# A delta-rule recurrence with a gated MLP: transfers planned through one shared queue, and matmuls of zeros in TensorE's gaps before the first gate tile

## The chip, the core and the metric

The kernel runs on one core of a Trainium2 chip. The core has TensorE (PE, matmuls; its weight loads are shown apart as PEld), VectorE (DVE), ScalarE (ACT), GpSimd (POOL) and SyncE (SP), which here issues every transfer. Each engine runs its own list of instructions in order, and semaphores tie the lists together. The metric is the device time of one execution in microseconds. Three runs of the kernel before took 659.91, 661.75 and 661.90 us, a median of 661.75 us.

## The reference

For each of 32 heads a 48 by 48 state is carried over 768 tokens (a delta rule with normalized keys), and what it gives goes through a gated MLP:

```python
for t in range(S):                       # q, k, v: (4, 8, 768, 48), beta: (4, 8, 768)
    kt, vt, bt = (k_n[:, :, t], v[:, :, t], beta[:, :, t, None])
    y[:, :, t] = np.einsum('bhd,bhde->bhe', q[:, :, t], state)
    v_old = np.einsum('bhde,bhd->bhe', state, kt)
    state = state + bt[:, :, :, None] * np.einsum('bhd,bhe->bhde', kt, vt - v_old)
x = attn_out.transpose(0, 2, 1, 3).reshape(B * S, H * D)      # 3072 x 384
gate = 1.0 / (1.0 + np.exp(-(x @ w_gate)))                    # 384 x 1536
return (gate * (x @ w_val)) @ w_out                           # 1536 x 384
```

## The kernel before

The tokens are cut into 12 groups `g` of 64 (times 4 batches: 256 rows of the MLP). A group's recurrence is done by blocks. `gram` (L250, tile pg) multiplies keys with keys, and ACT copies the blocks out (G at L258, L at L263). `norms` (L199 to L232) is a chain of some twenty small DVE instructions that gives the keys' norms and the tile mq. `solve` or, for groups 0 and 1, `solve_halves` (L315) inverts a triangular system by a long DVE chain. For these two groups the halves are joined by two sets of 64 tiny matmuls, pz and pm (`joining`, L354): pz needs the DVE transposition into mt (L342), ACT copies pz out (`keep_z`, L365), pm multiplies again, and DVE subtracts pm from mt (L346). Then come three PE steps (pu at L406, pk at L399, pu again), with copies of the state rows su by DVE and ACT between them (L412, L414). Then come yy (L434, L437), the copies ys (L446, L448), the transposition pt (L476) and the copies xx (L482, L484) that feed the MLP. ACT also scales the values by mq (`scale_v`, L238, 16 instructions a group).

The MLP works on 144 tiles: 12 groups by 12 slices `f` of 128 columns of the hidden layer. A gate tile is 18 matmuls of 128x256 (`gate_val`, L494). ACT, DVE, ACT and DVE turn it into two halves h, and six matmuls of 128x384 (`outp`, L530) add it into po. The order of tiles is group 0 up to slice 5, group 1 whole, the rest of group 0, then the groups in turn.

The weights come as 36 pieces of 384 KB. Each piece, once it has landed, is converted by two ACT instructions (L165 and L170, tile raw), one DVE instruction (L182, tile u), one ACT cast (L187) and one DVE subtraction (L192, tile w). A piece is loaded (`load_piece`, L155) only when POOL has copied one word out of the piece six places before it (`mark`, L175), which waits for that piece's L170. All 36 are converted once and kept.

What order the engines' lists have is set by a planner in the kernel (`schedule`, L737). Every step is a task with an engine, a cost in ns, the tasks it waits for, and buffers it takes and frees. The planner goes through the tasks by the earliest start on an engine, takes among those that could start at nearly the same time the one with the longest chain behind it, and keeps its own clock. The instructions are then issued by planned start. A transfer is a task of SP: before, it was planned to land 2500 ns plus its size over 380 after it was issued, whatever else was on the way. PE tasks before the first gate tile were planned at 2.1 times their cost (`COLD`, L795).

Of the kernel before, what the change touches and what calls it, by code (L numbers as in the profile page):

```python
# [12 lines left out]
F32 = mybir.dt.float32  # L13
# [43 lines left out]
def deltanet_gated_mlp(ctx: ExitStack, tc: tile.TileContext, kd, qd, kv, beta, words, out):  # L57
# [295 lines left out]

    def joining(g, n):  # L354

        pool, tag = (ps_aux, "aux") if g else (ps_gv, "gv")
        state[g][n] = out = pool.tile([128, CP, 32], F32, name=f"{n}_{g}", tag=tag)
        lhsT, rhs = (scratch[:, 0], mt) if n == "pz" else (scratch[:, 1], scratch[:, 2])
        for c in range(CP):
            for r in range(0, 128, 32):  # L360
                nc.tensor.matmul(out=out[r:r + 32, c], lhsT=lhsT[r:r + 32, c], rhs=rhs[r:r + 32, c], start=True, stop=True)  # L361
# [187 lines left out]
    PE, DVE, ACT, POOL, SP = range(5)  # L549
    tasks, by_name = [], {}  # L550

    def task(name, engine, cost, fn, after=(), take=(), free=(), late=0, lands=0):

        t = dict(name=name, engine=engine, cost=cost, fn=fn, after=[by_name[a] for a in after], take=take, free=free, late=late, lands=lands, n=len(tasks))
        assert name not in by_name, name
        by_name[name] = t
        tasks.append(t)
        return name
# [21 lines left out]
    pools = dict(aux=2, seq=2, gv=2, po=2, G=1, gp=1, X=1, mt=1, scratch=1, row=3, ys=1, sg=3, h=3, u=3, kv=2, L=2, xa=0, xb=1, mq=1)  # L580
# [19 lines left out]
    def load(g, what):  # L600
        k = f"kq{g % 2}"
        if what == "k":
            transfer(f"dk{g}", lambda: load_k(g), 2, 400000, has(f"pk{g - 2}", f"pp{g - 2}"))
        if what == "q":
            transfer(f"dq{g}", lambda: load_q(g), 2, 524288, has(f"yy{g - 2}"))
        if what == "v":
            transfer(f"dv{g}", lambda: load_rows(g, 1), 2, 400000, has(f"pd{g - 2}", f"less{g - 2}.1.1"))
        if what == "t":
            transfer(f"dt{g}", lambda: load_rows(g, 0), 1, 393216, has(f"pd{g - 2}"))

    HALF = {0, 1}

    def recurrence(g):
# [15 lines left out]
        if half:  # L629
            task(f"X{g}", POOL, 520, lambda: clear(g), take=("X",))  # L630
            task(f"ll{g}", ACT, 750, lambda: lower_left(g), [got[5]], take=("scratch",), free=("G",))
            gen = solve_halves(g)
            costs = [285, 418] * 2
            for j in range(15, 0, -1):
                costs += [160 + 1.05 * 2 * (8 - j // 2) * j] * 2
            h = steps(f"h{g}", DVE, gen, costs, [n[-2]])
            by_name[h[3]]["free"] = ("gp",)
            e = steps(f"x{g}", DVE, gen, [180, 180], [h[-1], f"X{g}"])
            task(f"mt{g}", DVE, 712, lambda: next(gen), e[-1:], take=("mt",), free=("X",))
            task(f"pz{g}", PE, 1500, lambda: joining(g, "pz"), [f"mt{g}", f"ll{g}"], take=("gv" if g == 0 else "aux",))  # L640
# [68 lines left out]
    def out_of(i):  # L709
# [3 lines left out]
        if ends(g, f):  # L713
            cleared.clear()
            for s in range(NSUB):
                cleared.append(f"part{s}" if f < NF - 1 else f"res{g}.{s}")
                if f < NF - 1:
                    task(f"part{s}", ACT, 480, lambda s=s: keep_part(g, s), [f"out{i}"], free=("po",))
                else:
                    task(f"res{g}.{s}", DVE if g == 0 else ACT, 560 if g == 0 else 480, lambda s=s: result(g, s), [f"out{i}"] + (has(f"part{s}") if g == 0 else []), take=("row",), free=("po",))  # L720
                    transfer(f"st{g}.{s}", lambda s=s: store(g, s), 2, 100000, [f"res{g}.{s}"], free=("row",))

    half = constants()
    second_half(half)
# [12 lines left out]
    def schedule():  # L737
# [13 lines left out]
        order = []  # L751
# [7 lines left out]
        while len(order) < len(tasks):  # L759
# [38 lines left out]
    begun = []

    def warm(t):  # L800
        begun.extend([t] * t["name"].startswith("gate"))
        return bool(begun)
# [50 lines left out]
```

## Time and profile before

| | before |
|---|---|
| the profiled execution's own time | 662.25 us |
| its span, first to last instruction | 660.5 us |
| PE busy | 610.7 us (92%) |
| DVE busy | 475.9 us (72%) |
| ACT busy | 324.8 us (49%) |
| the chain that ended last | PE 85%, DMA 5%, DVE 3%, issue 3%, ACT 2% |
| first gate tile starts | 67.83 us |
| share of the 16 DMA engines, 10 to 30 us | 1.0 |

The busy share is an average of two stages: the one before the first gate tile, in which PE mostly waits, and the one after it, in which PE hardly ever does. The granted clock of TensorE has a column in the profile (1.00 is 2.4 GHz, 0.50 is 1.2 GHz). "issue" is time in which an engine waited for nothing that the profile shows.

### The profile page before, as it was taken

How to read it: one execution, taken by the hardware profiler on the slowest of the kernel's cores; microseconds unless marked ns; L12 is line 12 of the kernel's file. 1: busy time of each engine (PE TensorE's matmuls, PEld its weight loads, DVE VectorE, ACT ScalarE, POOL GpSimd, SP SyncE). 2: the span in 40 equal slices, each digit the busy share in tenths (PEclk: the TensorE clock that was granted, in tenths of full speed). 3: DMA queues.
4: the chain of work that ended last, by engine and by line, in shares of the span. 5: the costliest groups of instructions: out<-in, count | busy, mean ns of one | idle time of the engine just before them, and what ended most of it. 6: DMA issues, size and time to landing. Idle time of an engine off the chain costs nothing.

```text
span 660.5 us, 24130 instructions
## 1 busy us (share of the span) xinstructions
PE 610.7 (92%) x10504; PEld 588.1 (89%) x10504; DVE 475.9 (72%) x1482; ACT 324.8 (49%) x881; POOL 14.8 (2%) x57
## 2 busy tenths in 40 slices
PE   5135899999999999999999999999999999999996
PEld 4134899988999999999999999999999999999996
DVE  4947599995985985985985985985985985984221
ACT  5599787245444445445445445445345345344321
POOL 5011000000000000000000000000000000000000
PEclk9999799998999999999999999999999999999999
DMA  9969320021211211211211211211211210100101
GB/s 261 289 201 319 93 79 2 1 67 34 58 32 45 58 30 48 58 47 30 58 50 28 57 51 28 58 48 29 57 51 27 58 51 3 26 1 4 25 1 24
DMA packets 17769, 41.06 MB, mean 62 GB/s; under 512 B 4224, under 2 KB 7296, under 8 KB 17664
## 3 DMA queue, kind: packets, MB, share of 16 engines
q1 hardware_dynamic: 17664, 39.53, 21.4%
q8 instruction: 82, 1.34, 0.8%
q14 instruction: 23, 0.19, 0.1%
HBM read 34.80 MB, written 4.72 MB: 60 GB/s over the span
## 4 chain that ended last, share of the span: by engine, by line
PE 85%; DMA 5%; DVE 3%; issue 3%; ACT 2%; SPq 1%; POOL 0%; ACTq 0%; POOLq 0%
PE gv L494 46%; PE po L530 24%; DMA raw<-in_words_dram 3%; PE pu L406 3%; PE pp L274 2%; PE pk L376 2%; PE yy L434 2%; PE yy L437 2%; PE pg L250 2%; PE pk L399 1%; PE pd L457 1%; DMA kv<-in_kv_dram 1%; PE pt L476 1%; DMA kqp<-in_qd_dram 1%; DVE X L305 1%
## 5 line engine op out<-in xcount | busy, mean ns | idle before, releaser
L494 PE MATMUL gv<-xx,w 128*128 128x256 f32 x2592 | 333.0, 284 | 1.4 <-DVE sg L504 1.4
L494 PEld LDWEIGHTS gv<-xx,w 128*128 128x128 f32 x2592 | 325.7, 191 | 3.0 <-DVE sg L504 2.1
L530 PE MATMUL po<-w,h 128*128 128x384 f32 x864 | 181.5, 348 | 0.0
L530 PEld LDWEIGHTS po<-w,h 128*128 128x128 f32 x864 | 146.8, 189 | 3.6
L499 ACT ACTIVATE sg<-gv 128x256 f32<-128x256 f32 x144 | 55.0, 382 | 154.8 <-PE gv L494 154.7
L504 DVE TENSOR_TENSOR sg<-sg,gv 128x256 f32<-128x256 f32 x144 | 59.9, 416 | 81.5 <-ACT sg L499 81.2
L509 ACT CAST h<-sg 128x256 fp32r<-128x256 f32 x144 | 58.5, 407 | 93.7 <-DVE sg L504 92.8
L305 DVE TENSOR_TENSOR X<-X,tmp 128x126 f32<-128x126 f32 (+22 forms) x310 | 79.0, 255 | 9.2
L302 DVE TENSOR_TENSOR tmp<-X,gp 128x126 f32<-128x126 f32 (+22 forms) x310 | 78.2, 252 | 7.3
L514 DVE TENSOR_TENSOR h<-sg,h 128x256 fp32r<-128x256 f32 x144 | 60.0, 417 | 16.0 <-ACT h L509 15.1
L414 ACT COPY su<-pu 32x384 f32<-32x384 f32 x92 | 43.3, 471 | 18.8 <-PE pu L406 17.8
L238 ACT ACTIVATE kv<-kv,mq 128x48 f32<-128x48 f32 x192 | 46.8, 322 | 2.6 <-DVE mq L232 2.6
L279 DVE TENSOR_TENSOR kqp<-pp,pmask 64x512 f32<-64x512 f32 x48 | 32.0, 685 | 2.2 <-PE pp L274 1.9
L258 ACT COPY G<-pg 32x256 f32<-32x256 f32 (+1 forms) x72 | 26.5, 368 | 10.7 <-PE pg L250 9.4
L199 DVE STREAM_TRANSPOSE gp<-G 128x1024 f32<-128x1024 f32 x12 | 14.9, 1245 | 19.4 <-ACT G L258 19.4
L387 DVE TENSOR_TENSOR R<-kv,pk 128x384 f32<-128x384 f32 x44 | 22.4, 550 | 6.0 <-PE pk L399 2.8
L170 ACT ACTIVATE raw<-raw 128x384 f32<-128x384 f32 x36 | 18.6, 547 | 8.5 <-DMA raw<-in_words_dram 8.4
L466 DVE TENSOR_TENSOR su<-su,pd 48x384 f32<-48x384 f32 x40 | 22.1, 552 | 0.8
L361 PE MATMUL pz<-mt,scratch 32*32 32x32 f32 x256 | 4.5, 237 | 18.7 <-DVE mq L232 9.8
L192 DVE TENSOR_TENSOR w<-u,w 128x384 fp32r<-128x384 f32 x36 | 19.2, 551 | 3.3 <-ACT w L187 3.2
L250 PE MATMUL pg<-kqp 48*64 48x64 f32 x768 | 17.0, 241 | 4.5 <-DMA kqp<-in_kd_dram 4.5
L361 PEld LDWEIGHTS pz<-mt,scratch 32*32 32x32 f32 x256 | 4.0, 150 | 19.3 <-issue 17.2
(88 smaller groups left out, 469.1 us busy)
## 6 DMA issues: line engine op xcount, KB each, us to landing
raw<-in_words_dram SPq DMA_DIRECT2D x36, 384.0 KB, 5.2
kv<-in_kv_dram SPq DMA_DIRECT2D x24, 384.0 KB, 3.9
kqp<-in_qd_dram SPq DMA_DIRECT2D x24, 256.0 KB, 4.0
kqp<-in_kd_dram SPq DMA_DIRECT2D x24, 192.0 KB, 3.6
out_dram<-ot SPq DMA_DIRECT2D x48, 96.0 KB, 2.2
beta<-in_beta_dram SPq DMA_DIRECT2D x12, 16.0 KB, 3.7
```

Source lines behind the costliest of these rows:

```text
L238: nc.scalar.activation(V[:, c], V[:, c], AF.Copy, scale=mq[:, c, 0:1])
L250: nc.tensor.matmul(out=pg[e][t:t + 64, j], lhsT=kq[r:r + D, x, j], rhs=kq[r:r + D, x, j], start=True, stop=True)
L279: nc.vector.tensor_tensor(out=kq[t:t + 64, sec], in0=pp[e][t:t + 64], in1=pmask[t:t + 64, e].unsqueeze(1).to_broadcast([64, J, C]), op=ALU ...
L302: nc.vector.tensor_tensor(out=tmp, in0=X[:, k:16, j:j + 1].to_broadcast([128, n, j]), in1=gp[:, j:j + 1, 0:j].to_broadcast([128, n, j]), o ...
L305: nc.vector.tensor_tensor(out=X[:, k:16, 0:j], in0=X[:, k:16, 0:j], in1=tmp, op=ALU.add)
L414: nc.scalar.copy(su[r:r + 32, 3 if x else e], pu[0][r:r + 32])
L494: nc.tensor.matmul(out=pg[:, o], lhsT=parts[w, f][:, a, k * 128:(k + 1) * 128], rhs=x[b][:, k], start=(k == 0 and q == 0), stop=(k == KC - ...
L499: nc.scalar.activation(h, st["gv", f][:, 0], AF.Sigmoid)
L504: nc.vector.tensor_tensor(out=h, in0=h, in1=st["gv", f][:, 1], op=ALU.mult)
L509: nc.scalar.copy(hh[:, 0], st["sg", f])
L514: nc.vector.tensor_tensor(out=hh[:, 1], in0=st["sg", f], in1=hh[:, 0].bitcast(F32), op=ALU.subtract)
L530: nc.tensor.matmul(out=po[s], lhsT=hh[:, a, ts], rhs=parts["o", f][:, w], start=begins(g, f) and q == 0, stop=ends(g, f) and q == 2)
```

## The change

In the planner, SP's transfers now share one queue: a transfer lands at the later of the queue's last landing and 2400 ns after its issue, plus a load time of its own (1150 ns for a piece of weights, 1900 for keys, 2200 for queries). The factor `COLD` is gone. Up to the task gate0, wherever PE's planned clock stands more than `ROOM` (450 ns) before the next PE task, the planner puts in fills of 230 ns each. A fill is a bf16 matmul of 128x512 with its own weight load, both operands a broadcast zero, into a PSUM buffer of the tag gv that the gate tiles use later. So that this buffer is free, only one gv buffer is planned until gate0, and group 0's pm is written over its pz. No arithmetic of the result changes.

```diff
+    def warm_up():
+        if not hot:
+            hot.append(ps_gv.tile([128, 512], F32, name="warm", tag="gv"))
+        z = zero.bitcast(BF16)[:, 0:1]
+        nc.tensor.matmul(out=hot[0], lhsT=z.to_broadcast([128, 128]), rhs=z.to_broadcast([128, 512]), start=True, stop=True)
...
-        pool, tag = (ps_aux, "aux") if g else (ps_gv, "gv")
-        state[g][n] = out = pool.tile([128, CP, 32], F32, name=f"{n}_{g}", tag=tag)
+        st = state[g]
+        if g == 0 and n == "pm":
+            st["pm"] = st["pz"]
...
-    def transfer(name, fn, count, size, after=(), take=(), free=()):
-        return task(name, SP, 430 * count, fn, after, take=take, free=free, lands=2500 + size / 380)
+    def transfer(name, fn, count, load, after=(), take=(), free=()):
+        return task(name, SP, 430 * count, fn, after, take=take, free=free, lands=2400, load=load)
...
-        transfer(f"w{n}", lambda: load_piece(n), 1, 393216, pre)
+        transfer(f"w{n}", lambda: load_piece(n), 1, 1150, pre)
...
+            if e == PE and filling:
+                clock[e] = max(clock[e], READY)
+                while at - clock[e] > ROOM:
+                    between.append(dict(name="warm", fn=warm_up, start=clock[e], engine=PE, done=clock[e] + FILL))
+                    clock[e] += FILL
+                if t["name"] == "gate0":
+                    tokens["gv"].append(at)
+                    filling.clear()
...
-            cost = t["cost"] * (COLD if e == PE and not warm(t) else 1)
+            cost = t["cost"]
...
-            t["end"] = at + cost + LATENCY[e] + t["lands"]
+            t["end"] = at + cost + LATENCY[e]
+            if e == SP:
+                t["end"] = moved[0] = max(moved[0], at + t["lands"]) + t["load"]
...
+    READY, FILL, ROOM = 2500, 230, 450
```

The planner's new costs move instructions on PE, ACT and DVE. There are 122 fills in all. On PE, around the joining of group 0 (pg is group 1's gram, pu the first step after the joining), the list before was:

```order
L250 MATMUL pg_1_285<-kqp_77 64x64
L361 MATMUL pz_445<-mt,scratch 32x32 x64
L361 MATMUL pm_542<-scratch 32x32 x64
L406 MATMUL pu_0_0_649<-kv_126,mt 32x48 x2
L406 MATMUL pu_0_1_650<-kv_126,mt 32x48 x2
```

and PE's list at the same place is now this, with a pair of rows for each fill (47 between pg and pz, then 4 and 4):

```order
L259 MATMUL pg_1_304<-kqp_77 64x64
L201 LDWEIGHTS zero
L201 MATMUL warm<-zero 128x512
...
L375 MATMUL pz_492<-mt,scratch 32x32 x64
L201 LDWEIGHTS zero
L201 MATMUL warm<-zero 128x512
...
L375 MATMUL pz_492<-scratch 32x32 x64
```

The matmuls of the kernel stand in the same sequence; 55 fills stand among those shown. Before pz the list has 6, 13 and 47 of them; between the first pu and pk (L399 before, L413 now) there are 28, then 7 and 7, and at last 1 and 5 before group 1's pz. On ACT, ahead of the copy of group 0's pz into scratch, the list before ended with these rows (raw_6 to raw_9 are pieces of weights, kv_0 the values that are scaled):

```order
L170 ACTIVATE raw_6_321<-raw_6_321 128x384
...
L170 ACTIVATE raw_4_218<-raw_4_218 128x384
L165 ACTIVATE raw_4_218<-raw_4_218 128x384
L263 COPY L_1_283<-pg_1_0_284 32x256
L170 ACTIVATE raw_8_340<-raw_8_340 128x384
L170 ACTIVATE raw_9_348<-raw_9_348 128x384
...
L165 ACTIVATE raw_7_333<-raw_7_333 128x384
L238 ACTIVATE kv_0_126<-kv_0_126,mq_0_443 128x48 x16
L365 COPY scratch_86<-pz_0_445 128x512
```

and ACT's list before that copy is now:

```order
L165 ACTIVATE raw_4_231<-raw_4_231 128x384
L272 COPY L_1_302<-pg_1_1_304 32x256
L247 ACTIVATE kv_0_126<-kv_0_126,mq_0_490 128x48 x8
L379 COPY scratch_86<-pz_0_492 128x512
L247 ACTIVATE kv_0_126<-kv_0_126,mq_0_490 128x48 x8
L187 CAST w_0_657<-u_0_645 128x384
L322 ACTIVATE scratch_86<-G_1_301,under_85 128x16x16
L187 CAST w_1_697<-u_1_651 128x384
L428 COPY su_79<-pu_0_0_0_662 32x384 x2
L170 ACTIVATE raw_6_344<-raw_6_344 128x384
```

Pieces 6, 7, 8 and 9 are no longer converted ahead of the copy of pz but after the copies of su, and half of the scaling stands behind it. On DVE, around the subtraction of pm from mt (the row that writes mt), the list before was:

```order
L182 SCALAR_TENSOR_TENSOR u_1_535<-raw_1_134 128x384
L199 STREAM_TRANSPOSE gp_1_538<-G_1_282 128x1024
L203 TENSOR_SCALAR n1_1_610<-gp_1_538 128x32
...
L224 TENSOR_TENSOR nt_1_612<-m_1_614 128x32
L346 TENSOR_TENSOR mt_78<-mt_78,pm_0_542 128x512
L227 RECIPROCAL gam_1_647<-nt_1_612 128x32
```

and DVE's list there is now:

```order
L182 SCALAR_TENSOR_TENSOR u_1_651<-raw_1_141 128x384
L355 TENSOR_TENSOR mt_78<-mt_78,pz_0_492 128x512
L208 STREAM_TRANSPOSE gp_1_660<-G_1_301 128x1024
L212 TENSOR_SCALAR n1_1_702<-gp_1_660 128x32
...
L233 TENSOR_TENSOR nt_1_706<-m_1_706 128x32
L236 RECIPROCAL gam_1_751<-nt_1_704 128x32
```

The first 15 instructions of group 1's norms, which stood before the subtraction, now stand behind it and ahead of the copy of su. On SP the transfers stand in the same sequence up to piece 11; where a task had been planned elsewhere (piece 10 ahead of piece 12, the queries of group 2 after piece 26) it moves by a few places.

## Rows read from the trace of the kernel before

**Rows 1.** The page, part 1: busy time, share and instructions of PE.
```profile
PE 610.7 (92%) x10504; PEld 588.1 (89%) x10504; DVE 475.9 (72%) x1482; ACT 324.8 (49%) x881; POOL 14.8 (2%) x57
```

**Rows 2.** PE before gate0: start, length, line, tile, count [idle <-releaser].
```profile
6.71 1.90 PE L376 MATMUL pk<-su,kqp 48*64 48x48 f32 x62
...
11.21 1.87 PE L274 MATMUL pp<-kqp 48*64 48x64 f32 x59 [0.80 <-DMA kqp<-in_qd_dram]
...
12.88 2.42 PE L250 MATMUL pg<-kqp 48*64 48x64 f32 x63
25.09 1.50 PE L361 MATMUL pz<-mt,scratch 32*32 32x32 f32 x94 [9.78 <-DVE mq L232]
31.40 0.74 PE L361 MATMUL pz<-mt,scratch 32*32 32x32 f32 x34 [4.81 <-issue]
38.77 1.94 PE L361 MATMUL pm<-scratch 32*32 32x32 f32 x128 [6.63 <-ACT scratch L365]
...
45.83 1.99 PE L399 MATMUL pk<-su,L 32*32 32x48 f32 x64 [2.82 <-ACT su L414]
...
53.98 2.06 PE L434 MATMUL yy<-su,kqp 48*64 48x48 f32 x64 [3.50 <-ACT su L414]
55.97 1.95 PE L437 MATMUL yy<-su,kqp 128*64 128x48 f32 x32
...
67.49 0.42 PE L361 MATMUL pz<-mt,scratch 32*32 32x32 f32 x11 [2.18 <-issue]
67.83 4.21 PE L494 MATMUL gv<-xx,w 128*128 128x256 f32 x18
```

**Rows 3.** ACT before gate0, the same columns.
```profile
20.89 0.53 ACT L170 ACTIVATE raw<-raw 128x384 f32<-128x384 f32 x1
27.68 0.55 ACT L170 ACTIVATE raw<-raw 128x384 f32<-128x384 f32 x1 [6.25 <-DMA raw<-in_words_dram]
...
34.41 3.70 ACT L238 ACTIVATE kv<-kv,mq 128x48 f32<-128x48 f32 x16
38.13 0.59 ACT L365 COPY scratch<-pz 128x512 f32<-128x512 f32 x1
...
60.22 0.46 ACT L448 COPY ys<-yy 128x384 f32<-128x384 f32 x1
```

**Rows 4.** DVE around the subtraction of pm, the same columns.
```profile
29.39 1.24 DVE L199 STREAM_TRANSPOSE gp<-G 128x1024 f32<-128x1024 f32 x1
...
33.68 0.19 DVE L224 TENSOR_TENSOR nt<-m 128x32 f32<-128x32 f32 x1
40.77 0.69 DVE L346 TENSOR_TENSOR mt<-mt,pm 128x512 f32<-128x512 f32 x1 [6.89 <-PE pm L361]
...
43.11 1.14 DVE L412 COPY su<-pu 32x384 f32<-32x384 f32 x2
```

**Rows 5.** Stretches: length, busy PE, PEld, DVE, ACT, POOL, PEclk, DMA share, GB/s.
```profile
54.00:56.00 2.00, 2.00 (x66) 1.91 (x66) 1.69 (x9) 1.51 (x4) 0.17 (x1) 1.00 1.00 395
...
66.00:68.00 2.00, 0.51 (x12) 0.45 (x11) 0.00 (x0) 0.91 (x5) 0.00 (x0) 0.50 0.98 265
...
72.00:74.00 2.00, 2.00 (x153) 1.96 (x156) 1.16 (x3) 1.83 (x5) 0.12 (x1) 0.72 0.00 0
```

**Rows 6.** PE after gate0, the columns of the second group.
```profile
85.97 0.88 PE L406 MATMUL pu<-R,mt 32*32 32x48 f32 x64
...
90.15 1.15 PE L434 MATMUL yy<-su,kqp 48*64 48x48 f32 x64
91.23 1.14 PE L437 MATMUL yy<-su,kqp 128*64 128x48 f32 x32
...
98.36 4.48 PE L494 MATMUL gv<-xx,w 128*128 128x256 f32 x36
```

**Rows 7.** DMA queues, 28.5 to 29 us: packets, MB, share of 16 engines.
```profile
q8 instruction: 1, 0.02, 13.7%
```

**Rows 8.** A stretch of ten us after gate0, the columns of the fifth group.
```profile
90.00:100.00 10.00, 10.00 (x154) 9.76 (x154) 9.84 (x23) 7.78 (x21) 0.00 (x0) 1.00 0.18 55
```

More of the change, by code (lines that the diff above doesn't have):

```diff
@@ L192, in weight_lo @@
         nc.vector.tensor_tensor(out=t[:, 1], in0=us[n].bitcast(F32), in1=t[:, 0].bitcast(F32), op=ALU.subtract)
+    hot = []
+    def warm_up():
[3 more added lines that the diff above has]
+        nc.tensor.matmul(out=hot[0], lhsT=z.to_broadcast([128, 128]), rhs=z.to_broadcast([128, 512]), start=True, stop=True)
     def norms(g):
@@ L354, in joining @@
     def joining(g, n):
-        pool, tag = (ps_aux, "aux") if g else (ps_gv, "gv")
-        state[g][n] = out = pool.tile([128, CP, 32], F32, name=f"{n}_{g}", tag=tag)
+        st = state[g]
+        if g == 0 and n == "pm":
+            st["pm"] = st["pz"]
+        else:
+            pool, tag = (ps_aux, "aux") if g else (ps_gv, "gv")
+            st[n] = pool.tile([128, CP, 32], F32, name=f"{n}_{g}", tag=tag)
+        out = st[n]
         lhsT, rhs = (scratch[:, 0], mt) if n == "pz" else (scratch[:, 1], scratch[:, 2])
@@ L550, in deltanet_gated_mlp, with task @@
     tasks, by_name = [], {}
-    def task(name, engine, cost, fn, after=(), take=(), free=(), late=0, lands=0):
-        t = dict(name=name, engine=engine, cost=cost, fn=fn, after=[by_name[a] for a in after], take=take, free=free, late=late, lands=lands, n=len(tasks))
+    def task(name, engine, cost, fn, after=(), take=(), free=(), late=0, lands=0, load=0):
+        t = dict(name=name, engine=engine, cost=cost, fn=fn, after=[by_name[a] for a in after], take=take, free=free, late=late, lands=lands, load=load, n=len(tasks))
         assert name not in by_name, name
@@ L575, in steps @@
         return names
-    def transfer(name, fn, count, size, after=(), take=(), free=()):
-        return task(name, SP, 430 * count, fn, after, take=take, free=free, lands=2500 + size / 380)
-    pools = dict(aux=2, seq=2, gv=2, po=2, G=1, gp=1, X=1, mt=1, scratch=1, row=3, ys=1, sg=3, h=3, u=3, kv=2, L=2, xa=0, xb=1, mq=1)
+    def transfer(name, fn, count, load, after=(), take=(), free=()):
+        return task(name, SP, 430 * count, fn, after, take=take, free=free, lands=2400, load=load)
+    pools = dict(aux=2, seq=2, gv=1, po=2, G=1, gp=1, X=1, mt=1, scratch=1, row=3, ys=1, sg=3, h=3, u=3, kv=2, L=2, xa=0, xb=1, mq=1)
     def fetch(n):
@@ L602, in load @@
         if what == "k":
-            transfer(f"dk{g}", lambda: load_k(g), 2, 400000, has(f"pk{g - 2}", f"pp{g - 2}"))
+            transfer(f"dk{g}", lambda: load_k(g), 2, 1900, has(f"pk{g - 2}", f"pp{g - 2}"))
         if what == "q":
-            transfer(f"dq{g}", lambda: load_q(g), 2, 524288, has(f"yy{g - 2}"))
+            transfer(f"dq{g}", lambda: load_q(g), 2, 2200, has(f"yy{g - 2}"))
         if what == "v":
-            transfer(f"dv{g}", lambda: load_rows(g, 1), 2, 400000, has(f"pd{g - 2}", f"less{g - 2}.1.1"))
+            transfer(f"dv{g}", lambda: load_rows(g, 1), 2, 1350, has(f"pd{g - 2}", f"less{g - 2}.1.1"))
         if what == "t":
-            transfer(f"dt{g}", lambda: load_rows(g, 0), 1, 393216, has(f"pd{g - 2}"))
+            transfer(f"dt{g}", lambda: load_rows(g, 0), 1, 1150, has(f"pd{g - 2}"))
     HALF = {0, 1}
@@ L641, in recurrence @@
             task(f"D{g}", DVE, 706, lambda: next(gen), [f"mt{g}"])
-            task(f"z{g}", ACT, 590, lambda: keep_z(g), [f"pz{g}"], free=("gv" if g == 0 else "aux",))
-            task(f"pm{g}", PE, 1300, lambda: joining(g, "pm"), [f"z{g}", f"D{g}"], take=("gv" if g == 0 else "aux",))
+            task(f"z{g}", ACT, 590, lambda: keep_z(g), [f"pz{g}"], free=("aux",) if g else ())
+            task(f"pm{g}", PE, 1300, lambda: joining(g, "pm"), [f"z{g}", f"D{g}"], take=("aux",) if g else ())
             task(f"T{g}", DVE, 685, lambda: next(gen), [f"pm{g}"], free=("gv" if g == 0 else "aux", "scratch") + (("xa",) if g == max(HALF) else ()))
@@ L720, in out_of @@
                     task(f"res{g}.{s}", DVE if g == 0 else ACT, 560 if g == 0 else 480, lambda s=s: result(g, s), [f"out{i}"] + (has(f"part{s}") if g == 0 else []), take=("row",), free=("po",))
-                    transfer(f"st{g}.{s}", lambda s=s: store(g, s), 2, 100000, [f"res{g}.{s}"], free=("row",))
+                    transfer(f"st{g}.{s}", lambda s=s: store(g, s), 2, 600, [f"res{g}.{s}"], free=("row",))
     half = constants()
@@ L744, in schedule @@
         for t in reversed(tasks):
-            t["level"] = t["late"] + max([(0 if b["engine"] == t["engine"] else LATENCY[t["engine"]] + t["lands"]) + b["level"] for b in t["then"]] or [0]) + t["cost"]
-        clock = [0.0] * 5
+            t["level"] = t["late"] + max([(0 if b["engine"] == t["engine"] else LATENCY[t["engine"]] + t["lands"] + t["load"]) + b["level"] for b in t["then"]] or [0]) + t["cost"]
+        clock, moved = [0.0] * 5, [0.0]
         tokens = {p: [0.0] * n for p, n in pools.items()}
@@ L750, in schedule @@
         when = {}
-        order = []
+        order, between, filling = [], [], [True]
         def release(t):
@@ L792, in schedule @@
                     release(b)
-        return sorted(order, key=lambda t: t["start"])
-    COLD = 2.1
+        return sorted(order + between, key=lambda t: t["start"])
+    READY, FILL, ROOM = 2500, 230, 450
     FROM_PSUM = set("G z T m less u s y xh xl sig prod part res".split())
     SLACK = {PE: 300, DVE: 150, ACT: 150, POOL: 0, SP: 0}
[L798 to L802, printed above, removed]
     EN = mybir.EngineType
```

## The prediction

> **What bounds the kernel now.** I read the page's busy shares first, then PE's instructions in order of time up to the first gate tile, then those of ACT and DVE over the same stretch, and at last the busy time and the clock by stretches. The page gives PE 92% of the span, so 660.5 - 610.7 = 49.8 us of PE's time are idle [rows 1]. In the order of time nearly all of that lies before gate0, which starts at 67.83 [rows 2]. After it PE is full, and DVE nearly so (9.84 of 10 us), with ACT at 7.78 [rows 8]. So the change can only win in the first 68 us, and it keeps what it wins only if DVE and ACT come forward as far as PE does.
>
> In that stretch one thread leads to gate0: pz, its copy, pm, the subtraction on DVE, three steps with copies of su, yy, ys, pt, xx. Three delays stand on it. First, pz stops after 94 of its 128 instructions and goes on 4.81 us later; nothing that the profile shows released it [rows 2]. One block of instructions for an engine is carried at 28.5 to 29 us, in that very gap, while the DMA engines are full [rows 7]; I read the stop as PE waiting for its own code. Second, ACT waits 6.25 us for a piece of weights that had been planned to land earlier, and then works through conversions and the scaling, so that it copies pz at 38.13, 6 us after pz ended at 31.40 + 0.74 = 32.14 [rows 2, 3]. Behind that DVE waits 6.89 us for pm [rows 4]. Third, the clock. The column says 1.00 at 54 to 56 us and 0.50 at 66 to 68 [rows 5], but yy takes 2.06 + 1.95 us there and 1.15 + 1.14 later [rows 2, 6]: PE was at 1.2 GHz in the first stretch already, and the column shows the upper level only because nothing had been recorded yet. Gate0 takes 4.21 us, where two tiles later take 4.48 [rows 2, 6]. After PE had worked without a gap from 67.5 on, the clock came back at about 73 [rows 2, 5].
>
> **The fills.** None is in the trace of before. The nearest rows are gate tiles: 4.48 / 36 = 0.124 us for 256 columns at the upper clock, 4.21 / 18 = 0.234 at the lower [rows 2, 6]. A fill has 512 columns, so I take 0.25 and 0.47 us. The lower bound is one 256-column matmul, 0.124. Before the first keys land PE has nothing to do, so the first 6 cost nothing. Pk ended at 8.6 [rows 2] and 13 fills follow. At the rise near 73 PE had worked without a gap since 67.5, and here it has done so since the first keys; so I let the clock come up a few fills in: 4 at 0.47 and 9 at 0.25 end at 12.7, while pp started at 11.2. That is 1.5 us late, but pp and pg then take some 1.2 us each where they took 1.9 and 2.4, so pg ends near 15, as before. The 47 take 11.8 us, to 26.8, where pz could start at 25.09: 1.7 us of overfill, which costs only if pz does not stop anyway. The Trainium skill, "TensorE: Matmul & The Clock Gate", section "Wait — 56ns, not 53.3ns?", gives 215.7 ns for N = 512 warm; by that the 47 would end at 25.1 and not be late. No row of this case shows it.
>
> **pz.** Counting each matmul instruction with its weight load as a pair, the stop before came after 64 + 64 + 64 + 64 + 94 = 350 pairs. With 66 fills ahead, the 350th pair is now the 28th of pz. If code comes in blocks of fixed size the stop falls in pz again. The transfers ahead of it are issued in the same sequence, so I take the same end, 31.4. Then 100 instructions at 1.50 / 94 = 0.016 us remain: pz ends at 33.0.
>
> **ACT.** Between group 1's copies, which end near 18 with pg unmoved, and pz's copy there stand now 10 conversions of 0.47 us (0.53 alone [rows 3]; two in a row overlap), four short copies of some 0.36 and, once mq is there at 25.0, half of the scaling (3.70 / 2 = 1.85). ACT is free at 27, so it waits only for pz and copies at 33.0 to 33.6, 5.1 us earlier than 38.13.
>
> **pm and the subtraction.** PE idles near 5 us in the stop, so I price the next steps at the lower clock: 4 fills (1.9, beside the copy), pm 1.94 from 34.9, and the subtraction at 36.9 instead of 40.77, 3.9 us earlier.
>
> **Norms, the part that gives it back.** The 15 instructions that DVE did from 29.39 to 33.87 while it waited now stand behind the subtraction: 4.5 us. With the 1.65 us between the end of the subtraction (41.46) and su (43.11) [rows 4] the copy of su starts at 36.9 + 0.7 + 4.5 + 1.65 = 43.7, 0.6 us later than before. The 28 fills (7.0 us) lie in this wait of PE, and end near 46.5. So pk starts at about 46.5, against 45.83: nothing is won up to here.
>
> **From pk to gate0** the gain comes. PE has been kept at work since 31.4, so I price at the upper clock: pk 0.9 for 1.99 (by the 0.88 of a step of equal size), pu 0.9 for about 2, yy 2.3 for 4.0 [rows 2, 6]. Less work of DVE and two sets of 7 fills (1.75 each) lie between; DVE needs 1.0 for the subtraction, 1.6 for 7 solver steps and 1.1 for su. ACT has 21 conversions (9.9 us, and some 0.6 of waiting for pieces) after its first su, so its second su ends near 52.2. Yy then ends at 54.6. ACT copies ys after 7 more conversions, near 55.5 to 56, against 60.22 [rows 3]. Pt 0.6, xx on ACT (its turn comes after two copies of the state) to 58.2, DVE's second half and two subtractions of weights 1.5: gate0 starts at 59.8, 8.0 us earlier. It takes 2.3 instead of 4.21, 1.9 more. Together 9.9 us.
>
> **What is late next.** At its copy of xx ACT has done 12 conversions fewer than before (41 against 53): 5.6 us, plus 12 of 16 scalings, less two state copies, 7.4 us of debt, and it gets there only 5 us sooner. So ACT is behind in total work, and has 2.2 idle us in ten to pay from [rows 8]. The pieces from 18 up are wanted only in the second half of group 1, so I charge only 0.9 us. Group 1's pz stopped too, for 2.18 us [rows 2]; I leave that stop as it was. Sum: 9.9 - 0.9 = 9. The profiled execution took 662.25 us; 662.25 - 9 = 653.3. That execution is 0.5 above the median of the runs, so I predict 652.8.
>
> **Rivals.** *Pz does not stop.* For it: only one or two crossings of many stopped before. Against it: pz meets the same place at the same load. Then pz ends at 28.5, after the overfill; the subtraction at full clock comes about 5.5 to 6 us earlier still, and all behind it moves by as much, to a gain of 9 + 6 = 15 and 647 us. The Trainium skill, "Runtime: NRT & Kernel Launch", section "Instruction fetch mechanics", has the next block of 256 instructions fetched while the present one runs, with the crossing mostly hidden; by that rule this is the case to expect, and the 4.81 us of this trace speak against it. Chance 0.25.
>
> *The debt comes due.* DVE had 0.16 idle us in ten after gate0, and each wait of it for ACT's casts is lost for good [rows 8]. If conversions pushed behind gate0 hold up casts, the 7.4 us are paid in full during groups 0 and 1: a gain of 9.9 - 7.4 = 2.5, or nothing with another stop. Some 660 us. Chance 0.17.
>
> *Fills at half clock* (slower). If matmuls of zeros do not bring the clock up, a fill takes 0.47. The 13 end at 14.7, pp and pg at their old cost at 19, the 47 at 41, pz 43; fills and pm put the subtraction at 47, pu ends at 51, 28 fills at 64, and two sets of 7 add 3 each: gate0 at about 84, 16 us late, 678 us. It decides from where a fill takes more than its gap, 6.3 / 28 = 0.23 us in the longest one on the thread; at 0.30 us a mean the 122 have eaten the forecast's 9. Against it: the clock came up at 73 while PE worked without a gap [rows 2, 5], and the fills leave it none. Chance 0.08.
>
> **Chances and range.** The forecast 0.50, the others as above. What can be told from no change in this kernel is about 0.3%, 2 us. Faster: the forecast, the first rival, and most of half of the second: 0.82. Same: the other half, 0.10. Slower: 0.08. The forecast's own range is 649 to 657 (fill at 0.124 to 0.25, stops of 3 to 8 us). Eight in ten need both neighbours: 644 to 660.5.
>
> **What would show it.** Right: gate0 near 60; a gap marked "issue" inside group 0's pz, ending near 31; the copy of pz within 1 us of pz's end; 4.5 us of norms between the subtraction and su; yy near 2.3 us. Wrong: gate0 near 52 (no stop) or above 68 (fills); fills of 0.4 us and more behind 15 us; PE waiting for weights or DVE between gate0 and 150 us by more than 5 us in all.

## The result and the profile after

The changed kernel takes 654.57 us (median of 4 runs, 654.11 to 654.98), the kernel before beside it 661.83 us (4 runs). The ratio is 0.9897, with an interval of 0.9878 to 0.9916. The profiled execution took 654.68 us, its span is 652.6 us. The page's part 1 answers to [rows 1]: PE is busy 19.5 us longer, most of it fills (30.1 us of records at L201).

```profile
PE 630.2 (97%) x10618; PEld 591.3 (91%) x10626; DVE 475.4 (73%) x1482; ACT 323.3 (50%) x881; POOL 16.6 (3%) x57
```

PE's instructions in order of time, from the 47 fills to the first gate tile (start, length, line, tile, count, idle time with its releaser), answer to [rows 2]:

```profile
15.84 10.23 PE L201 MATMUL warm<-zero 128*128 128x512 bf16 x46 [0.16 <-issue]
26.00 1.29 PE L375 MATMUL pz<-mt,scratch 32*32 32x32 f32 x128
...
28.19 0.38 PE L375 MATMUL pz<-scratch 32*32 32x32 f32 x23
32.01 1.09 PE L375 MATMUL pz<-scratch 32*32 32x32 f32 x105 [3.43 <-issue]
...
42.91 0.88 PE L413 MATMUL pk<-su,L 32*32 32x48 f32 x64
...
49.31 1.25 PE L448 MATMUL yy<-su,kqp 48*64 48x48 f32 x64 [1.45 <-DVE tmp L343]
...
57.01 1.24 PE L375 MATMUL pz<-mt,scratch 32*32 32x32 f32 x123
62.03 0.32 PE L375 MATMUL pz<-mt,scratch 32*32 32x32 f32 x5 [3.78 <-issue]
62.27 4.21 PE L508 MATMUL gv<-xx,w 128*128 128x256 f32 x18
```

A fill takes 10.23 / 46 = 0.22 us. Pz of group 0 no longer stops. A stop of 3.43 us now stands in pm (32x32 matmuls that read scratch alone are pm, written over pz), 23 instructions in. Group 1's pz stops after 123 of 128 for 3.78 us, and gate0 behind it takes 4.21 us, the lower clock, as before. It starts 5.56 us earlier than in [rows 2].

ACT answers to [rows 3]:

```profile
27.33 0.58 ACT L379 COPY scratch<-pz 128x512 f32<-128x512 f32 x1 [0.38 <-PE pz L375]
...
48.30 0.96 ACT L428 COPY su<-pu 32x384 f32<-32x384 f32 x2
...
52.85 0.45 ACT L462 COPY ys<-yy 128x384 f32<-128x384 f32 x1
```

The copy of pz comes 10.8 us earlier and right behind pz; the wait of 6.25 us for a piece is gone from its way. DVE answers to [rows 4]:

```profile
33.20 0.69 DVE L355 TENSOR_TENSOR mt<-mt,pz 128x512 f32<-128x512 f32 x1 [3.76 <-issue]
33.80 1.24 DVE L208 STREAM_TRANSPOSE gp<-G 128x1024 f32<-128x1024 f32 x1
...
38.09 0.19 DVE L233 TENSOR_TENSOR nt<-m 128x32 f32<-128x32 f32 x1
...
40.01 1.14 DVE L426 COPY su<-pu 32x384 f32<-32x384 f32 x2
```

The norms stand behind the subtraction, 4.5 us of them. A stretch inside the stop of group 1's pz, with the columns of [rows 5], and the instruction queue from 18 to 19 us and from 58.5 to 59.5 us, which answers to [rows 7]:

```profile
60.00:62.00 2.00, 0.00 (x0) 0.00 (x0) 0.00 (x0) 0.00 (x0) 0.00 (x0) 0.63 1.00 314
```

```profile
q8 instruction: 1, 0.02, 8.4%
q8 instruction: 1, 0.02, 8.5%
```

Nothing computes for two us, the DMA engines are full, and one block of code began to be carried at 59.4, 2.6 us before PE went on. The blocks of q8 are PE's: over the whole run it carries 83 of them (82 before), and PE's matmuls and weight loads, 21252 with the unrecorded fills counted (21008 before), are 83.0 and 82.1 times 256. Ahead of group 0's pz a block was carried at 18.2, while the fills ran; in the trace of before none came between 12.8 and 28.8 us, though PE stood idle from 15.3 to 25.1.

The rest of the gain comes later. Gate1 starts 5.65 us earlier (69.05 against 74.70) and the last instruction ends 7.9 us earlier, so some 2.2 us are won behind gate1. Part of it lies in one stretch, here that of before, in which PE waited for four copies of su by ACT (0.59 + 3 x 0.23 us) and then worked at the lower clock:

```profile
150.00:160.00 10.00, 8.73 (x219) 7.44 (x218) 4.38 (x9) 4.30 (x11) 0.00 (x0) 0.83 0.19 43
```

and the same stretch after:

```profile
150.00:160.00 10.00, 10.00 (x247) 9.53 (x246) 5.88 (x19) 7.25 (x19) 0.00 (x0) 1.00 0.06 14
```

### The profile page after: what moved, and what is told of

Same layout as the page of the kernel before. It is cut to its first block, busy times and chain, and to the rows that moved or that the text cites. A ratio compares the mean times of both kernels' runs of the same rounds, so it can differ in the third digit from the quotient of the medians.

```text
span 652.6 us, 24378 instructions
## 1 busy us (share of the span) xinstructions
PE 630.2 (97%) x10618; PEld 591.3 (91%) x10626; DVE 475.4 (73%) x1482; ACT 323.3 (50%) x881; POOL 16.6 (3%) x57
## 4 chain that ended last, share of the span: by engine, by line
PE 85%; DMA 5%; DVE 4%; issue 3%; ACT 1%; SPq 0%; POOL 0%; ACTq 0%; POOLq 0%
PE gv L508 46%; PE po L544 23%; DMA raw<-in_words_dram 3%; PE pu L420 3%; PE yy L448 2%; PE yy L451 2%; PE pp L283 2%; PE pg L259 2%; PE pk L390 2%; PE pk L413 1%; DMA kv<-in_kv_dram 1%; PE pt L490 1%; PE pd L471 1%; DVE X L314 1%; DVE tmp L311 1%
## 5 line engine op out<-in xcount | busy, mean ns | idle before, releaser
L523 ACT CAST h<-sg 128x256 fp32r<-128x256 f32 x144 | 58.5, 406 | 89.6 <-DVE sg L518 88.9
L201 PE MATMUL warm<-zero 128*128 128x512 bf16 x114 | 30.1, 420 | 3.9 <-issue 2.8
L201 PEld LDWEIGHTS <-zero 128*128 128x128 bf16 x122 | 12.3, 106 | 17.8 <-issue 6.0
L187 ACT CAST w<-u 128x384 fp32r<-128x384 f32 x36 | 17.2, 511 | 6.1 <-DVE u L182 6.0
L420 PEld LDWEIGHTS pu<-R,mt 32*32 32x32 f32 x1408 | 16.4, 105 | 4.0 <-DVE R L401 2.3
```

Source lines behind the costliest of these rows:

```text
L201: nc.tensor.matmul(out=hot[0], lhsT=z.to_broadcast([128, 128]), rhs=z.to_broadcast([128, 512]), start=True, stop=True)
L420: nc.tensor.matmul(out=pu[0 if g else x][r:r + 32, j], lhsT=mt[r:r + 32, e * J + j], rhs=R[e][r:r + 32, j], start=True, stop=True)
L523: nc.scalar.copy(hh[:, 0], st["sg", f])
```

## The experiments

All ratios are to the kernel before on the same chip, with their intervals. The first four ran beside each other, then four more, then three, then one. The kernel before took 660.45 to 661.83 us from set to set, so between sets the ratios say more than the times.

### Without the fills

```diff
-        t["fn"]()
+        if t["name"] != "warm":
+            t["fn"]()
```

> The planner plans as in the changed kernel, but none of the 122 fills is issued; the order of all other instructions is that of the changed kernel. Theory A (the new order frees the copy of pz, the fills hold the clock and move the place at which PE runs out of code): pz stops again after 94 of its 128 instructions, to about 31.4; pk and pu of group 0 take near 2.0 us and yy 4.0; gate0 starts at 64 to 65 instead of 62.3, and the time is about 657. Rival (the fills are worth nothing, since DVE and ACT set the pace before gate0): gate0 within 0.5 us of 62.3 and a time of 654 to 655.

Measured: 655.15 us, ratio 0.9924 (0.9897 to 0.9950). PE:

```profile
25.07 1.50 PE L375 MATMUL pz<-mt,scratch 32*32 32x32 f32 x94 [9.77 <-DVE mq L241]
31.11 0.74 PE L375 MATMUL pz<-mt,scratch 32*32 32x32 f32 x34 [4.54 <-issue]
...
63.24 0.31 PE L375 MATMUL pz<-mt,scratch 32*32 32x32 f32 x11 [2.84 <-issue]
63.48 3.92 PE L508 MATMUL gv<-xx,w 128*128 128x256 f32 x18
```

The stop is back after 94 instructions, where before had it. Pt starts 3.6 us later than with the fills, but gate1 only 0.57 us (69.62 against 69.05): group 1's pz stops a shorter time, 2.84 us. The order of events is that of theory A, the time is nearer to the rival's. By the ratios (0.9924 against 0.9897) the fills are worth 1.8 us, by the times 0.6, and the intervals don't separate either from nothing. The new order without fills keeps 5.0 of the 6.8 us.

### The fills alone, with the old rule for transfers

```diff
-        return task(name, SP, 430 * count, fn, after, take=take, free=free, lands=2400, load=load)
+        return task(name, SP, 430 * count, fn, after, take=take, free=free, lands=2500 + SIZE[load] / 380)
...
-                t["end"] = moved[0] = max(moved[0], at + t["lands"]) + t["load"]
+                t["end"] = at + cost + t["lands"]
```

> The fills stay (about 120 of them), but the planner lands each transfer by the old rule, on its own, 2500 ns plus size over 380 after its issue. Pieces 6 to 9 are again converted ahead of the copy of pz. Theory A: ACT waits 6 us for piece 6 and copies pz near 35 instead of 27.3; what is left of the gain is the clock, some 2 to 4 us, so 658 to 660. Rival (the whole gain is the clock that the fills hold up): 654 to 655, with pz copied late but nothing behind it later.

Measured: 659.90 us, ratio 0.9999 (0.9975 to 1.0023). ACT, then PE:

```profile
27.53 0.56 ACT L170 ACTIVATE raw<-raw 128x384 f32<-128x384 f32 x1 [6.32 <-DMA raw<-in_words_dram]
...
36.17 0.59 ACT L379 COPY scratch<-pz 128x512 f32<-128x512 f32 x1
```

```profile
61.49 1.25 PE L375 MATMUL pz<-mt,scratch 32*32 32x32 f32 x125
68.77 0.31 PE L375 MATMUL pz<-mt,scratch 32*32 32x32 f32 x3 [6.03 <-issue]
```

With the old rule the fills win nothing. ACT again stands 6.32 us before a piece that has not landed and copies pz at 36.17. Group 1's pz begins 2.0 us earlier than in [rows 2], and its stop of 6.03 us takes that back. With the run before this one it follows that the gain needs the planner's queue for transfers, and that the queue gives most of it without the fills. `COLD` was gone in both runs; what its removal does by itself was not tested.

### Each of the 47 fills cut in two

Their 512 columns are worked in two matmuls of 256, so that 47 more instructions stand ahead of pz.

```diff
+        if t["name"] == "warm" and last == "gram1":
+            warm_up(256)
+            warm_up(256)
```

> The 47 fills of 512 columns ahead of group 0's pz become 94 of 256 columns: the same columns, 47 more pairs of weight load and matmul. Theory A (PE runs out of code after a fixed number of instructions, here pair 478): the stop of 3.4 us leaves pm and comes after about 109 of pz's 128 instructions, near 27.6 us; it still ends at 31 to 32; time within 1.5 us of 654.6. Rival (the stop has to do with pm or with a moment of time): it stays in pm, after about 23 instructions.

Measured: 655.23 us, ratio 0.9934 (0.9916 to 0.9953). PE:

```profile
25.16 1.12 PE L375 MATMUL pz<-mt,scratch 32*32 32x32 f32 x109
28.21 0.53 PE L375 MATMUL pz<-mt,scratch 32*32 32x32 f32 x19 [1.93 <-issue]
...
53.72 0.85 PE L375 MATMUL pz<-mt,scratch 32*32 32x32 f32 x76
58.79 0.96 PE L375 MATMUL pz<-mt,scratch 32*32 32x32 f32 x52 [4.21 <-issue]
```

Pairs of a matmul and its weight load, counted from the start: before stopped at 256 + 94 = 350; the changed kernel in pm at 478 (322 to pz's start, 128, 4 fills, then 23 or 24); here 322 + 47 + 109 = 478; group 1's stop moved up by the same 47 (123 to 76). The stop follows the count and not the tile: this is theory A. Group 1's stop comes at 1115 by this count, 5 x 128 - 3 pairs after 478, and in before at 987, 128 earlier; so stops lie 128 pairs apart within three, and what the three are is open. Theory A's end of the stop, 31 to 32, was missed: it ended at 28.21.

### Pieces 6 to 11 loaded only after the copy of group 0's pz

```diff
-        nc.gpsimd.tensor_copy(out=raw[n][0:1, 0:1, 0], in_=raw[n - AHEAD][0:1, 0:1, 1])
+        if n < 2 * AHEAD:
+            nc.gpsimd.tensor_copy(out=raw[n][0:1, 0:1, 0], in_=scratch[0:1, 2, 0, 0:1].bitcast(U32))
```

> Pieces 6 to 11 of the weights are loaded only after the copy of group 0's pz (at about 27.3), so the DMA engines are nearly idle when PE needs its next block of code; ACT first wants piece 6 near 37.7. Theory A (the block is late because the DMA engines are full): the stop in pm falls from 3.4 us to 1.5 or less, pm ends 2 to 3 us earlier, and the time is 651 to 653.5, less what the second stop in group 1's pz takes back. Rival (a block takes that long whatever the load): the stop stays at 3 us or more and the time at 654 to 655.5.

Measured: 653.97 us, ratio 0.9913 (0.9894 to 0.9933). PE:

```profile
29.43 1.09 PE L378 MATMUL pz<-scratch 32*32 32x32 f32 x105 [0.68 <-issue]
...
31.43 0.44 PE L423 MATMUL pu<-kv,mt 32*32 32x48 f32 x19
34.91 0.70 PE L423 MATMUL pu<-kv,mt 32*32 32x48 f32 x45 [3.05 <-issue]
```

With few transfers on the way (the DMA engines' share is 0.04 from 26 to 28 us, against 1.01 in the changed kernel) the stop in pm falls from 3.43 to 0.68 us, and the next one, when the held pieces all come, grows from 0.17 to 3.05. A stop's length goes with what the DMA engines carry then, as theory A has it; the time lies between the two theories.

### The changed kernel once more

> The changed kernel once more, as the base for the kernels beside it. Both theories: 654.6 us within 1.5, pz of group 1 stops after 123 of its 128 instructions, gate0 starts near 62.3 and takes 4.2 us.

Measured: 653.39 us (651.02 to 657.43), ratio 0.9881 (0.9828 to 0.9934). Its trace has a span of 649.0 us, 3.6 less than the first, with 3.24 us for the same stop, and gate0 at 59.35 against 62.27, so that the expected gate0 was missed. Two executions of one program differ here by 3 us before gate0, so a difference of 1 or 2 us between single traces says little.

### Group 1's norms first

```diff
+    k = plan.index(named["T0"])
+    plan[k:k] = norms1
```

(the list `norms1` holds the norms' first 14 instructions; the 28 fills are cut to 12)

> Group 1's norms (14 instructions of DVE, 4.5 us) are put ahead of group 0's subtraction in DVE's order, and the 28 fills behind the first pu are cut to 12. By my prediction's step on the norms they stand on the path: su is copied near 36.3 instead of 40.0, pk starts near 39 instead of 42.9, and yy comes 3.5 to 4 us earlier. Theory A (the stop of group 1's pz sets the end of the stage: a block of code that comes when the full queues let it, near 61 to 62): gate0 starts only 0 to 1 us earlier than 62.3, its time stays 4.2 us, and the whole takes 653.5 to 655. Theory B (the norms are the bound, and the stop only follows what is ahead of it): gate0 starts near 58.5, and the whole takes 650.5 to 651.5.

Measured: 657.14 us, ratio 0.9933 (0.9908 to 0.9957). PE, then ACT:

```profile
50.10 1.95 PE L448 MATMUL yy<-su,kqp 48*64 48x48 f32 x62 [5.10 <-ACT su L428]
...
64.60 1.65 PE L508 MATMUL gv<-xx,w 128*128 128x256 f32 x6 [4.72 <-issue]
```

```profile
49.09 0.96 ACT L428 COPY su<-pu 32x384 f32<-32x384 f32 x2
```

DVE copied su at 37.18, 2.8 us earlier, and pk began at 39.75, 3.2 us earlier. But ACT's second copy of su came at 49.09, against 48.30: it stands behind 21 conversions, one of which waited 1.64 us for a piece. PE idled 5.10 us, yy took 1.95 us at the lower clock, and the stop, 16 pairs on with the 16 fills gone, fell into gate0. Both theories missed: the norms were not the bound, ACT's list was. Two things were changed at once here, so how much of the loss is due to the fills that were cut is not shown.

### Gate0 ahead of group 1's pz

```diff
+    plan.remove(named["pz1"])
+    plan.insert(plan.index(named["gate0"]) + 1, named["pz1"])
```

> Gate0 is issued ahead of group 1's pz in PE's order, nothing else is changed. Theory A (the stop of 3.8 us stands on the path, and it is what drops the clock): gate0's 18 instructions do not cross a block's end; gate0 starts near 57.2 behind the fills, takes 2.3 instead of 4.2 us, the stop falls in pz 18 pairs earlier (after some 105) and is shorter by gate0's time, or ends at the same 62; gate1 comes 1 to 4 us earlier than 69.05, and the whole takes 651 to 653.5. Theory B (the inputs of gate0 are what is late, and the stop hides behind them): gate0 stays near 61 to 62, and the whole takes 654 to 655.

Measured: 653.51 us, ratio 0.9880 (0.9844 to 0.9915). PE:

```profile
55.02 2.49 PE L508 MATMUL gv<-xx,w 128*128 128x256 f32 x18
...
60.59 0.39 PE L375 MATMUL pz<-mt,scratch 32*32 32x32 f32 x23 [2.07 <-issue]
...
66.51 3.33 PE L508 MATMUL gv<-xx,w 128*128 128x256 f32 x18
```

Gate0 starts 4.3 us ahead of the run beside it, at the upper clock, and the stop is shorter. But pz comes no earlier, its stop ends at 60.59, and behind it the clock is down: gate1 starts at 66.51, against 65.41 there. What gate0 won, gate1 lost.

### Pieces from the 17th on, and group 2's loads, held until group 1's pz is copied

```diff
+        if n == HOLD:
+            nc.gpsimd.tensor_copy(out=raw[n][0:1, 0:1, 0], in_=scratch[0:1, 2, 0, 0:1].bitcast(U32))
```

> The pieces of weights from the 17th on, and group 2's first loads behind them, are issued only after the copy of group 1's pz, so that the queues have run dry when PE crosses into the next block of code in that pz. Seven conversions move behind that copy on ACT with them. Theory A (the length of a stop is the time that a block of code needs through full queues): the stop of 3.78 us falls to 0.5 to 1.2 us, gate0 starts near 59.3 at 2.3 to 4.2 us, and the whole takes 650.5 to 652.5. Theory B (a stop is PE's own decoding, whatever the queues carry): the stop stays 3.4 to 4.2 us, and the whole takes 654 to 656.

Measured: 654.40 us, ratio 0.9898 (0.9857 to 0.9939). PE, a stretch, and PE's waits from 100 to 165 us (total, times, longest):

```profile
52.59 0.25 PE L378 MATMUL pz<-mt,scratch 32*32 32x32 f32 x5 [0.65 <-issue]
52.78 2.40 PE L511 MATMUL gv<-xx,w 128*128 128x256 f32 x18
...
63.86 1.03 PE L423 MATMUL pu<-R,mt 32*32 32x48 f32 x41 [2.02 <-issue]
```

```profile
130.00:140.00 10.00, 8.09 (x113) 7.25 (x112) 9.50 (x32) 5.70 (x22) 0.00 (x0) 1.00 0.14 35
```

```profile
PE gv L511 <- DVE sg L521: 2.8, 5, 1.1
```

Theory A was right on the stop: 0.65 us, and gate0 at the upper clock, 6.6 us ahead of the run beside it. It was wrong on the time; its profiled execution took 651.20 us and that of the run beside it 651.02. Three later stops (1.47, 2.02 and 0.86 us) come when the held pieces do, and then DVE is full and PE waits. In both traces of the changed kernel the last row's wait is shorter:

```profile
PE gv L508 <- DVE sg L518: 1.5, 3, 1.0
```

### Four pieces on the way instead of six

```diff
-            pre = [task(f"mark{n}", POOL, 170, lambda: mark(n), [f"rescale{n - AHEAD}"])]
+            pre = [task(f"mark{n}", POOL, 170, lambda: mark(n), [f"rescale{n - PACE}"])]
```

(PACE is 4, and group 2's loads stand behind piece 19)

> A piece of weights is asked for when the one four before it has been converted, instead of six before, and group 2's first loads come after piece 19; PE's order is that of the changed kernel, ACT takes five conversions later. Theory A (a stop lasts as long as a block of code needs through what is queued in front of it): with four pieces of 0.39 MB in flight instead of six, and without group 2's loads, the stop of group 1's pz falls from 3.2 to 3.8 us to between 1 and 2.5, gate0 starts at 57 to 60. Of that at most half is kept, since DVE has under 1 us idle in ten from 80 to 140: 652 to 654 us beside 653.5 to 654.6 for the changed kernel. Theory B (the length of a stop does not go by what is queued): stop 3.2 to 4, gate0 at 59 to 62.5, 653.5 to 655.

Measured: 652.14 us, ratio 0.9873 (0.9848 to 0.9899), the lowest of all, though its interval overlaps that of the changed kernel. PE:

```profile
29.21 1.09 PE L375 MATMUL pz<-scratch 32*32 32x32 f32 x105 [1.17 <-issue]
...
57.44 0.25 PE L375 MATMUL pz<-mt,scratch 32*32 32x32 f32 x5 [3.34 <-issue]
```

The stop in pm fell to 1.17 us, where the DMA engines' share was 0.13 and less from 26 to 30 us. Group 1's did not, against theory A's 1 to 2.5: the DMA engines were full there (a share of 1.03 to 1.04 from 50 to 60 us). Gate0 and the time lie within theory A's ranges all the same, the time also 1.4 us below theory B's.

### The held pieces without fills

```diff
-        t["fn"]()
+        if t["name"] != "warm":
+            t["fn"]()
```

> The kernel that holds pieces from the 17th on until group 1's pz is copied, with all fills left out (they are planned, so everything else keeps its place). There the stop that swallowed the fills' gain is down to 0.65 us. Theory A (the fills raise the clock and win what the stop then takes back): without them yy takes 2.0 + 1.9 us instead of 1.25 + 1.14, pk and pu 1.5 to 2.0 instead of 0.9, gate0 starts 3 to 5 us later than 52.8; at the end 1 to 2.5 us of it are left, 655 to 657. Theory B (DVE, full from 80 to 140 us, sets the end, and the fills only give PE a longer wait behind it): gate0 later by as much, but the whole within 1 us of 654.4.

Measured: 655.52 us, ratio 0.9913 (0.9894 to 0.9932), inside theory A's range and 0.1 us above theory B's, and the intervals with and without fills overlap. The profiled execution took 660.53 us, 5 more than the median, so its rows show the manner and not the size:

```profile
57.23 2.40 PE L511 MATMUL gv<-xx,w 128*128 128x256 f32 x18
...
64.24 0.51 PE L378 MATMUL pm<-scratch 32*32 32x32 f32 x29 [3.64 <-issue]
```

Gate0 comes 4.5 us later than with fills, and about 1 us of it is left at the end, which is not clear of the noise.

### The held pieces let go one by one

```diff
+            nc.gpsimd.tensor_copy(out=raw[n][0:1, 0:1, 0], in_=raw[n - (AHEAD if n < HOLD else PACE)][0:1, 0:1, 1])
```

(PACE is 3, and group 2's loads stand behind piece 20)

> As the kernel that holds pieces from the 17th on, but after the release each piece waits for the conversion of the third before it, and group 2's loads for piece 20; the wish is a version that beats both. Theory A (the four later stops there, 1.47, 0.65, 2.02 and 0.86 us, and the lower clock behind the longest come from the release of all pieces at once): they fall to 2 us in all, gate2 takes 2.4 instead of 3.52 us, and the whole takes 650.5 to 653. Theory B (DVE, full from 80 to 140, sets the end): the stops fall, PE waits for DVE longer by as much, and the whole takes 653.5 to 655.

Measured: 653.14 us, ratio 0.9883 (0.9860 to 0.9905). PE, three stretches, and PE's waits from 100 to 165 us:

```profile
53.81 2.40 PE L511 MATMUL gv<-xx,w 128*128 128x256 f32 x18
...
84.73 4.47 PE L511 MATMUL gv<-xx,w 128*128 128x256 f32 x36
```

```profile
110.00:120.00 10.00, 8.54 (x120) 8.09 (x118) 9.65 (x31) 3.97 (x10) 0.00 (x0) 1.00 0.05 10
120.00:130.00 10.00, 8.18 (x112) 7.40 (x112) 9.69 (x33) 4.32 (x14) 0.00 (x0) 1.00 0.24 75
130.00:140.00 10.00, 8.31 (x112) 7.50 (x112) 9.57 (x31) 4.77 (x18) 0.00 (x0) 1.00 0.17 41
```

```profile
PE gv L511 <- DVE sg L521: 4.3, 5, 1.9
```

All stops from group 1's pz to 75 us sum to 2.1 us. Group 1's first tiles start at 84.73, 8.4 us earlier than in the first trace of the changed kernel. From 110 to 140 PE then idles 5.0 us with DVE at 9.6 to 9.7 of ten (in the two traces of the changed kernel it idles 1.6 and 1.9 us there, with DVE at 9.4 to 9.5): DVE works through group 2's solver between the gate tiles. The waits are those of theory B; the time lies between the two theories.

### Group 2's solver earlier

```diff
-            task(f"T{g}", DVE, 712, lambda: next(gen), [h[-1]], take=("mt",), free=("X",))
+            task(f"T{g}", DVE, 712, lambda: next(gen), [h[-1]], take=("mt",), free=("X",), late=4000 if g == 2 else 0)
```

> As the kernel with held and paced pieces (653.14 us), with one addition: the end of group 2's solver is due 4 us earlier in the planner, which puts group 2's first products on PE two gate tiles ahead of where they stood, and DVE's norms and solver steps of group 2 with them, into the stretch from 80 to 98 us in which DVE had 5 us idle in 18. Theory B, to which the last runs point (from 98 to 140 us DVE, at 9.6 to 9.7 of 10, sets the end, so what is won before gate0 counts only if DVE's work comes forward with it): PE's waits for DVE between 100 and 165 us fall from 5.2 to 2 to 3.5, and the whole takes 650 to 652, the first to beat the changed kernel. Theory A (PE's stops before 75 us are all that counts): nothing more to win, 652.5 to 654.

Measured: 656.23 us, ratio 0.9923 (0.9897 to 0.9950), a miss. Group 2's pg started at 92.72 us, only 1.1 us earlier, since the stage before it ran later, and further on PE waited longer:

```profile
133.77 3.06 PE L511 MATMUL gv<-xx,w 128*128 128x256 f32 x18 [2.59 <-DVE tmp L314]
```

Between two of the products that gate tiles need (127.19 and 133.22 us) DVE works without a pause on solver steps and on weights that came late. PE's waits for DVE from 100 to 165 us sum to 5.1 us, against 5.2 without this edit and 2 to 3.5 expected. That DVE's order is the next bound is what the waits of the runs with held pieces point to; no run here has relieved DVE and so shown it.

## Why the prediction was right, and which steps were not

The time was right (652.8 forecast, 654.57 measured). The reason was right in part: ACT's list let pz be copied early, and without the new rule for transfers nothing is won (0.9999). But by the forecast's own sum nothing was won up to pk, and 5.8 of its 9.9 us came from the upper clock that the fills bring (pk 1.1, pu 1.1, yy 1.7, gate0 1.9). The runs give the new order 5.0 us without any fill, and the fills at most some 1.8, not clear of nothing. That the sum still came out within 2 us is luck: several terms were off and made up for each other. Forecast were 8.0 us up to gate0, 1.9 in gate0 and -0.9 behind it; measured were 5.6, nothing and 2.2.

| step | forecast, us | measured, us |
|---|---|---|
| pz stops after its 28th | 31.4 | does not stop |
| ACT copies pz | 33.0 | 27.33 |
| subtraction | 36.9 | 33.20 |
| norms between the subtraction and su | 4.5 | 4.5 |
| su copied by DVE | 43.7 | 40.01 |
| pk | 46.5 | 42.91 |
| ys | 55.5 to 56 | 52.85 |
| stop of group 1's pz | 2.18 | 3.78 |
| gate0 starts | 59.8 | 62.27 |
| gate0 takes | 2.3 | 4.21 |
| behind gate0 | loses 0.9 | wins some 2.2 |
| all | 9 | 7.9 by the spans, 7.6 by the profiled executions |

*The stop in pz.* The step failed on the place; that PE waits for a block of its code holds. I counted to the 350th pair, now the 28th of pz. But every 128th pair is a crossing, and only those stop PE at which the next block has not come. At the 28th of pz it had: it was carried at 18.2, while the 47 fills ran. Time alone does not explain this, for PE stood idle for 9.78 us ahead of pz in before, 34 pairs past the crossing at pair 222, and the block began to be carried only at 28.9. The same holds in the two runs without fills (28.6 and 27.6), while in all with fills it was carried at 16.9 to 18.6. And in the run with the old rule for transfers, PE waited 7.71 us for ACT some hundred pairs past the crossing at 350, the block was carried at 28.6, inside that wait, and pm did not stop. So it looks as if the next block is asked for only when PE has worked some way into the present one, and the fills carried PE there; that is read from these traces, and no run was made for it. The stop moved one block on, to the 478th pair, which comes 128 pairs later, nearly all of them tiny. So the prediction's first rival, "pz does not stop", came half true: its 647 us fell with the stop in pm and the next one. The Trainium skill, "Runtime: NRT & Kernel Launch", section "Instruction fetch mechanics", has code come in blocks of 256 instructions, with the crossing mostly hidden. The block's size agrees with stops 128 pairs apart and with the count of q8's blocks. Most of the 83 crossings cost nothing here too (the changed kernel's first trace marks no idle time of PE as "issue" behind 75 us), but single ones cost up to 6.03 us.

*The norms* stood behind the subtraction with the price that I gave. But I took them for what gives the gain back; moved out of the way (with fewer fills), they won nothing, because ACT's second copy of su comes no earlier.

*Group 1's pz.* I left its stop at 2.18 us and let gate0 run at the upper clock. Measured, the stop was 3.78 us, ended at 62.03, PE idled through it, and gate0 took 4.21 us. This step cost 1.6 + 1.9 us, and it took back the 3 us by which ys was earlier than forecast. It also swallows the fills: pk, pu and yy did get shorter as forecast (0.88, 0.88 and 2.3 us), and yet gate1 comes only 0.57 us later without them.

*The debt of ACT.* I charged 0.9 us. No such loss shows: PE is busy 86.27 us from 76 to 165, where before had 85.98. The forecast took DVE's and ACT's idle time after gate0 from one stretch of ten us [rows 8], 0.16 and 2.2 in ten; from 76 to 165 us of before it is 12.0 and 35.5 of 89, which is 1.4 and 4.0 in ten, room enough to pay. Nor did nearly all of PE's idle time lie before gate0: 41.4 of the 49.8 us did. The gain behind gate0 was not forecast. The stretch shown above holds some of it; the rest was not traced.

*Fills at half clock* did not happen where it counted: the first 6 took 2.74 us and the next 12 recorded ones 4.58, but from the 47 on a fill took 0.22, close to the 0.25 of the forecast.

What stays open: why the length of a stop differs between 3.2 and 3.8 us for the same program, what the removal of `COLD` does by itself, and whether DVE's list can be ordered so that an earlier gate0 is kept. None of the versions beats the changed kernel by more than its interval.

## What to carry to other kernels

A planner that lets each transfer land a fixed time after its issue puts an in-order engine before data that are not there; planning the transfers through one queue, which changes no arithmetic, gave most of the gain here (0.9924 of 0.9897 without fills), and without it the fills gave none. Before filling an engine's gaps, look at which wait ends the stage: time won ahead of a stall that ends by its own clock is lost in it. And when a stall is removed, look for the engine that is full further on: here some 6 us won before the first gate tile did not show in the time; behind it, DVE was at 9.5 to 9.7 of ten and PE's waits for it grew from 1.5 to 4.3 us.

## What the hardware showed that was not expected

- PE stops at a 128th pair of matmul and weight load if the next block of its code is late; stops lie 128 pairs apart within three. Behind 47 fills (10.2 us) such a crossing cost nothing; 128 pairs of 32x32 are worked in 1.3 us, and behind them it cost 3.43.
- Idle time does not bring the block by itself: before, PE stood idle 9.78 us and then stopped for 4.81 us all the same.
- The stop's length goes with the transfers: 0.65 and 0.68 us when pieces were held back, 1.9 to 4.8 in most stops with the DMA engines full, 6.03 at the most.
- The column of the granted clock is not to be trusted before a first change has been recorded: [rows 5] shows 1.00 for a stretch in which yy took 2.06 us, against 1.25 with fills ahead.
